# Lightning attention, a Fourier mix and an MLP on one core: the sign of the weights by a bit operation of VectorE, copies of the first batch in another order, and another figure behind the second batch's folds

## The chip, the core and the metric

The kernel runs on one core of a Trainium2 chip. The core has a matrix engine (TensorE, PE in the profile), an elementwise engine (VectorE, DVE), an engine for functions and copies (ScalarE, ACT), a general engine (GpSimd, POOL), and a queue engine that issues DMA transfers (SyncE, SP). Each engine takes its own instructions in a fixed order; semaphores hold an instruction back until what it needs is there. The metric is the time of one execution on the device, in microseconds (us); lower is better. The kernel before has a median of 832.36 us over 6 runs, from 827.09 to 833.14.

## The reference: what is computed

Four sequences (batches) of 768 positions pass through two blocks. The first is lightning attention with 8 heads of 64 elements: within a block of positions, scores with a decay by distance, and between blocks a state that is carried on.

```python
intra = np.einsum('bhic,bhjc->bhij', qb, kb) * Dmask[None]
intra = np.einsum('bhij,bhjd->bhid', intra, vb)
inter = np.einsum('bhid,bhde->bhie', qb * lam_pow[None], kv_state)
out[:, :, sl] = intra + inter
```

Its result, 768 rows of 512 elements for each batch, goes through a Fourier transform along both axes, of which the real part is added. Then come a normalisation of each row, an MLP from 512 to 2048 and back to 512, and a sum:

```python
mixed = np.real(np.fft.fft(np.fft.fft(x, axis=1), axis=2)).astype(np.float32)
u = x + mixed
un = (u - mu) / np.sqrt(var + 1e-06)
ch = np.maximum(un @ w_ch1, 0.0) @ w_ch2
return (u + ch).astype(np.float32)
```

The two weights arrive as float64 numbers (they are scaled by a float64 number when they are made), all else as float32. All matrix products here are in float32.

## The kernel before

**Attention.** For each batch `b` there are six chunks of 128 positions. `attn_in` loads k, q and v of a chunk, turns k and q with TensorE (L274, L279), and ScalarE copies them out of PSUM as kT and qT (L276, L281). `attn_out` makes the scores (L298), multiplies them by the decay on VectorE (`sc`, L302), and adds the state's part (L328) and the scores' part (L332) into one PSUM tile `po`. ScalarE copies it to `oT` (L335), and the function `back` turns it once more (L348) into rows, which ScalarE copies to `x` in two halves (L350, L351, the second half of the columns in reversed order).

The Fourier mix needs each row together with the row that mirrors it. For batches 1 to 3 the rows are written to memory (`xa`, `xb`) and gathered back in mirrored order by GpSimd (`mirror_a`, `mirror_b`). For batch 0 (`TURNED`) the mirrored rows are made on the chip: ScalarE copies `po` reversed along the positions into `oTs` (a tile named `ds`, L386, and one column at L392), and `mirrored` sends that through `back` too. `LEADS = (0,)` names the batch whose mix runs beside the next batch's attention.

**The Fourier mix.** `fold_a` and `fold_b` (L418 to L476) use the symmetries: sums and differences of mirrored rows and columns on VectorE, in place, in tiles `fe` and `fo`. The products with the tables of cosines and sines are L508 (along the positions) and L521 to L526 (along the columns). VectorE adds them to x (L588 to L592); then the norm (L538 to L556) gives `un`, which is turned by TensorE (L561) for the first four groups of rows or by VectorE for the others.

**The MLP.** A group is 256 rows. The first four groups (`PLAIN`) use `mlp`: the first product is L625 (four matmuls for each of 16 column blocks `fc`), a relu alternates between VectorE (L631, odd `fc`) and ScalarE (L633, even `fc`), and the second product is L639, one matmul for each `fc` and each 128 rows. Both products write to PSUM tiles of a pool `pm` with three buffers. The first three groups are done in two halves of `fc`, the second after the second half of the weights has come. The other eight groups are done in pairs from about 440 us on (`late`, L712 and L759).

**The weights.** `load_weights` takes one of 32 tiles of 128 × 512. It loads the 64-bit numbers as pairs of 32-bit words (`raw`) and makes float32 of them: the power of two out of the top 16 bits, `top`, which lie 8 bytes apart (L217 on VectorE, L218 on ScalarE), the sign (L216 on ScalarE, and a product L220 on VectorE), and the fraction (L222, L224). L225 multiplies the two. The order is: first half of w1 (tiles 0 to 7), first half of w2 (8 to 15), then the second halves.

**The order of the work.** Every part is a generator that yields an estimated time. `weave` and `beside` interleave two of them in proportion to these times: attention of batch 0 beside the first weights; the mix of batch 0 beside the attention of batch 1 and more weights; then the first MLP halves beside the weights and `fr`, the rest of the front end (attention and mix of batches 1 to 3). A larger yield in `fr` means that more MLP work is put in at that place. A scheduler then orders each engine's instructions, except those marked with `tc.keep_in_program_order`. TensorE takes its matmuls in the order so fixed: one that waits holds up all behind it.

```python
half = [[mlp(b, g, h * FO // 2, (h + 1) * FO // 2) for b, g in PLAIN[:3]] for h in range(2)]
fr = chain([att1, fft_ln(1)] + [front(b) for b in range(2, B)])
...
run(beside(beside(chain(half[0]), t_half, w, 0.5 * NW), t_half + 0.5 * NW, fr, t_rest * t_half / t_back))
run(w)
back = chain(half[1] + [mlp(*PLAIN[3])])
run(weave(fr, back, (t_back - t_half) / (t_rest - t_rest * t_half / t_back)))
```

Of the kernel before, what the change touches and what calls it, by code (L numbers as in the profile page):

```python
# [76 lines left out]
def kernel(  # L77
# [24 lines left out]
    BLK = [128, S // 4 + 1 - 128]  # L102
# [12 lines left out]
    def front_pool(name, bufs):  # L115
        return front_end.enter_context(tc.tile_pool(name=name, bufs=bufs, side="left"))
# [8 lines left out]
    fp = front_pool("fp", 1)  # L125
    np_ = front_pool("np", 2)
    ep = front_pool("ep", 2)
# [63 lines left out]
    WP = 512  # L191
# [8 lines left out]
    def load_weights(dst, src):  # L200

        if src.dtype == F32:
            nc.sync.dma_start(dst, src)
            return
        raw = hp_.tile([128, 2 * WP], U32, tag="hr", name=f"raw{cnt[0]}")
        e = ep.tile([128, 2 * WP], U16, tag="e", name=f"e{cnt[0]}")
        pw, sg = e[:, 0:WP], e[:, WP:2 * WP].bitcast(BF16)
        cnt[0] += 1
        nc.sync.dma_start(raw, src.bitcast(U32))
        lo, hi = raw[:, 0:2 * WP:2], raw[:, 1:2 * WP:2]  # L210
        top = raw.bitcast(U16)[:, 3:4 * WP:4]
        d = dst.bitcast(U32)


        pin = tc.keep_in_program_order if late_words else lambda i: i
        pin(nc.scalar.activation(sg, top.bitcast(I16), AF.Sign))  # L216
        pin(nc.vector.tensor_scalar(pw, top, 0x7FF0, None, op0=ALU.bitwise_and))  # L217
        nc.scalar.activation(pw, pw, AF.Relu, bias=cvt[:, 0:1], scale=8.0)  # L218
        p = pw.bitcast(BF16)
        nc.vector.tensor_tensor(p, p, sg, op=ALU.mult)  # L220

        pin(nc.vector.tensor_scalar(d, hi, 0x000FFFFF, 0x00100000, op0=ALU.bitwise_and, op1=ALU.bitwise_or))  # L222
        del late_words[0:1]
        nc.vector.scalar_tensor_tensor(dst, lo, 2.0 ** -32, d, op0=ALU.mult, op1=ALU.add)  # L224
        nc.vector.scalar_tensor_tensor(dst, dst, 2.0 ** -20, p, op0=ALU.mult, op1=ALU.mult)  # L225
# [28 lines left out]
    ins, oTs, eo = {}, {}, {}  # L254
    LEADS = (0,)
    TURNED = (0,)
    first = const.tile([128, HP, 1], F32, name="first")
# [31 lines left out]
    def attn_out(b, c, head):  # L289
        kT, qT, qs, kd, vt = ins.pop((b, c))  # L290
        last = c == NC - 1


        mm = nc.tensor.matmul
        pss = [psum_a([C, HP, C]) for _ in range(2)]
        for hp in range(HP):
            for hi in range(2):
                mm(pss[hi][:, hp, :], lhsT=kT[HD[hi], hp, :], rhs=qT[HD[hi], hp, :], start=True, stop=True)  # L298
        sc = []
        for hi in range(2):  # L300
            t = new(at, [C, HP, C], "sc", bufs=3)
            nc.vector.tensor_tensor(t, pss[hi], decay[:, hi::2, :], op=ALU.mult)  # L302
            sc.append(t)
        if last and b - 1 in LEADS:
            mirror_a(b, pin=True)
        yield 1.5


        s_old, s_new = st[(c + 1) % 2], st[c % 2]
        if not last:  # L310
            pu = psum_a([128, HP, D])
            for hp in range(HP):
                for hi in range(2):
                    h = 2 * hp + hi
                    mm(pu[HD[hi], hp, :], lhsT=kd[:, h, :], rhs=vt[:, h, :], start=True, stop=True)  # L315
            if c == 0:
                nc.vector.tensor_copy(s_new, pu)
            else:
                nc.gpsimd.tensor_tensor(s_new, s_old, spow.broadcast_to([128, HP, D]), op=ALU.mult)
                nc.vector.tensor_tensor(s_new, s_new, pu, op=ALU.add)  # L320
            yield 0.9


        po = psum_a([128, HP, C])
        if c > 0:
            for hp in range(HP):
                for hi in range(2):
                    mm(po[HD[hi], hp, :], lhsT=s_old[HD[hi], hp, :], rhs=qs[HD[hi], hp, :],  # L328
                       start=(hp == 0), stop=False, skip_group_check=True)
        for hp in range(HP):  # L330
            for hi in range(2):
                mm(po[HD[hi], hp, :], lhsT=vt[:, 2 * hp + hi, :], rhs=sc[hi][:, hp, :],  # L332
                   start=(c == 0 and hp == 0), stop=(hp == HP - 1), skip_group_check=True)
        oT = new(at, [128, HP, C], "oT")
        nc.scalar.copy(oT, po)  # L335
        if b in TURNED:

            if c == 0:
                nc.scalar.copy(first, po[:, :, 0:1])
            elif c > 1:  # L340
                nc.scalar.copy(oTs[b][:, :, 0:1], po[:, :, 0:1])
        yield 2.0
        yield from head

        def back(oT, x, n=128):
            px = psum_a([C, HP, 128])
            for hp in range(HP):
                nc.tensor.transpose(px[:, hp, :], oT[:, hp, :], ident)  # L348
            px = px.rearrange("p h e -> p (h e)")
            nc.scalar.copy(x[0:n, 0:HM], px[0:n, 0:HM])  # L350
            nc.scalar.copy(x[0:n, HM:DM], px[0:n, DM - 1:HM - 1:-1])  # L351

        if b not in TURNED:
            x = xn_[b, c] = new(xp, [C, DM], "x") if c < HC else new(xn, [C, DM], "xn")
            back(oT, x)
            if c == 0:
                xd[b] = (dram.tile([S - 256, DM], F32, name=f"xa{b}"), dram.tile([257, DM], F32, name=f"xb{b}"))
                nc.scalar.dma_start(xd[b][1][256:257], x[0:1])
            elif not last:
                nc.scalar.dma_start(xd[b][0][(c - 1) * C:c * C], x)  # L360
            if c >= NC - 2:
                nc.scalar.dma_start(xd[b][1][(c - NC + 2) * C:(c - NC + 3) * C], x)
            if c == NC - 2 and b - 1 not in LEADS:
                mirror_a(b)
            elif last:
                mirror_b(b)
            yield 1.7
            return


        if c == 2:
            eo[b] = new_eo()

        def mirrored(m):
            if m < HC:
                back(oTs[b], eo[b][HC - 1 - m][1][:, 1, 0:DM], BLK[HC - 1 - m])
            else:
                u = xs[b, HC + NC - 1 - m] = new(xp, [128, DM], "x")
                back(oTs[b], u)

        if c > 1:
            mirrored(c - 1)
            yield 1.4
        if c > 0:
            oTs[b] = new(fp, [128, DM + 4], "ds")[:, 0:DM].rearrange("p (h c) -> p h c", h=HP)
            nc.scalar.copy(oTs[b][:, :, C - 1:0:-1], po[:, :, 1:C])  # L386
        if not last:
            x = xn_[b, c] = new(xp, [C, DM], "x") if c < HC else new(xn, [C, DM], "xn")
            back(oT, x)
            yield 1.7  # L390
        else:
            nc.scalar.copy(oTs[b][:, :, 0:1], first)  # L392
            mirrored(c)
            for t in range(HC):
                xs[b, t] = xn_.pop((b, t))
            yield 1.4
# [28 lines left out]
    def mirror_a(b, pin=False):  # L425

        xa = xd[b][0]

        eo[b] = new_eo()
        for a, n in enumerate(BLK):  # L430
            i = gather(out=eo[b][a][1][0:n, 1, 0:DM], out_offset=None, in_=xa[:, :], in_offset=row_of(a, n))
            if pin:

                tc.keep_in_program_order(i)
        for t in range(2, HC):
            u = xs[b, HC + t] = new(xp, [128, DM], "x")
# [46 lines left out]
    def fft_ln(b):  # L483
# [7 lines left out]
        if b in LEADS:  # L491
            yield from fold_a(b)
            yield from fold_b(b, sets)
            yield 2.0
        else:
            yield 1.0
            run(fold_a(b))
            yield 3.0
            run(fold_b(b, sets))
            yield 9.0  # L500


        for i in range(5):
            ps = psum_a([128, 2, NK])
            m = 128 if i < 4 else 1
# [72 lines left out]
        for t in (1, 2, 0):  # L578
# [7 lines left out]
            ds = new(fp, [128, 2 * (HM + 2)], "ds")  # L586
# [3 lines left out]
            u, v_ = xs[b, t], xs[b, HC + t]  # L590
# [219 lines left out]
    def run(gen):  # L810
        return sum(gen)
# [35 lines left out]
    back = chain(half[1] + [mlp(*PLAIN[3])])  # L847
# [47 lines left out]
```

## Time and profile before

| what | value |
|---|---|
| time, median of 6 runs | 832.36 us (827.09 to 833.14) |
| the profiled execution: its own time | 833.46 us |
| its span in the profile | 831.3 us |
| TensorE busy | 799.9 us, 96% |
| VectorE busy | 443.2 us, 53% |
| ScalarE busy | 182.7 us, 22% |
| GpSimd busy | 77.9 us, 9% |
| L216, the sign on ScalarE | 32 of 683 ns: 21.8 us |
| L220, the product on VectorE | 32 of 440 ns: 14.1 us |

The profile is of one execution. Its span is the time from the first to the last instruction; the execution's own time has 2.2 us more around it. A share is the busy time of an engine over the whole span; the slices of the span show where that time lies. A row of a group gives the source line, the engine, the operation, what it writes and reads, the shapes, how many there are, their busy time and the mean of one, and then how long the engine stood still just before them and what ended that. A float32 matmul leaves two records in the trace. The mean of one instruction holds its latency; where instructions follow one another, the distance from one start to the next is shorter, and it is that which fills an engine.

### The profile page before, as it was taken

The numbers are of one execution on the slowest core, as the hardware profiler recorded it, in microseconds if no ns is written. First come the engines' busy times: TensorE is split into PE (matmuls) and PEld (weight loads), VectorE is DVE, ScalarE is ACT, GpSimd is POOL, SyncE is SP. The second block draws the span as 40 slices with busy tenths as digits, with TensorE's granted clock in tenths as the row PEclk, the third lists the DMA queues.
The fourth block names the chain that finished last, engine by engine and source line by source line (L and its number), as shares of the span: only waits on it lengthen the run. The fifth ranks groups of instructions, "written<-read, shape, count | busy, mean of one in ns | idle before, by whom it ended". The sixth has DMA issues, their size and how long they took to land.

```text
span 831.3 us, 11682 instructions
## 1 busy us (share of the span) xinstructions
PE 799.9 (96%) x4608; PEld 636.4 (77%) x4608; DVE 443.2 (53%) x1030; ACT 182.7 (22%) x436; POOL 77.9 (9%) x102
## 2 busy tenths in 40 slices
PE   6889889999999999999999999999999999999998
PEld 5767765757675866767748888888888888888886
DVE  6889779856843582245895551156312561145411
ACT  3655443125530210222101210022001220012100
POOL 3112140012010110220100000000000000000000
PEclk9999999999999999999999999999999999999999
DMA  9966542247861128440442011100111001110010
GB/s 235 252 149 194 142 132 76 84 113 186 229 168 41 51 55 161 104 123 22 114 105 98 1 51 51 51 1 0 52 51 51 0 1 35 36 32 1 1 39 25
DMA packets 126684, 68.87 MB, mean 83 GB/s; under 512 B 111151, under 2 KB 112175, under 8 KB 126631
## 3 DMA queue, kind: packets, MB, share of 16 engines
q1 hardware_dynamic: 121488, 55.67, 26.5%
q0 software_dynamic: 2112, 6.69, 2.5%
q10 hardware_dynamic: 3030, 5.78, 2.0%
q8 instruction: 36, 0.59, 0.3%
q14 instruction: 18, 0.14, 0.1%
HBM read 48.72 MB, written 19.40 MB: 82 GB/s over the span
## 4 chain that ended last, share of the span: by engine, by line
PE 80%; DVE 10%; DMA 4%; issue 4%; ACT 1%; POOL 1%; SPq 0%; POOLq 0%; DVEq 0%; ACTq 0%
PE p L759 23%; PE p L712 23%; PE pm L639 10%; PE pm L625 7%; PE pa L508 3%; PE pa L332 3%; PE pa L298 3%; PE pa L328 2%; DMA x<-xb,ix 1%; PE pa L274 1%; PE pa L315 1%; PE pa L348 1%; DMA xb<-xn 1%; DVE stt L538 1%; PE pa L279 1%
## 5 line engine op out<-in xcount | busy, mean ns | idle before, releaser
L625 PE MATMUL pm<-ut,w 128*128 128x256 f32 x512 | 119.1, 382 | 0.2 <-DVE hr L631 0.2
L639 PE MATMUL pm<-w,hr 128*128 128x512 f32 x256 | 118.0, 605 | 1.3 <-DVE hr L631 1.3
L625 PEld LDWEIGHTS pm<-ut,w 128*128 128x128 f32 x512 | 94.4, 190 | 15.4 <-issue 3.1
L712 PE MATMUL p<-ur,w 128*128 128x256 f32 x384 | 93.8, 379 | 0.0
L639 PEld LDWEIGHTS pm<-w,hr 128*128 128x128 f32 x256 | 46.9, 191 | 51.0 <-issue 47.6
L712 PEld LDWEIGHTS p<-ur,w 128*128 128x128 f32 x384 | 73.0, 190 | 10.3 <-issue 0.5
L712 PE MATMUL p<-us,w1s 128*128 128x256 f32 x256 | 65.7, 379 | 0.0
L759 PE MATMUL p<-w,hs 128*128 128x256 f32 x256 | 58.0, 379 | 0.5 <-DVE y L780 0.5
L759 PE MATMUL p<-w,ha 128*128 128x256 f32 x256 | 57.9, 379 | 0.0
L759 PE MATMUL p<-w2s,hs 128*128 128x256 f32 x256 | 57.9, 379 | 0.0
L759 PEld LDWEIGHTS p<-w,hs 128*128 128x128 f32 x256 | 48.5, 190 | 7.5 <-DVE y L780 0.9
L759 PEld LDWEIGHTS p<-w,ha 128*128 128x128 f32 x256 | 48.6, 190 | 6.6
L759 PEld LDWEIGHTS p<-w2s,hs 128*128 128x128 f32 x256 | 48.6, 190 | 6.6
L712 PEld LDWEIGHTS p<-us,w1s 128*128 128x128 f32 x256 | 48.6, 190 | 6.6
L614 POOL DMA_INDIRECT out_dram<-y,ix x12 | 11.8, 987 | 408.5 <-DVE y L785 341.8
L739 ACT COPY ha<-p 128x256 f32<-128x256 f32 x32 | 11.9, 372 | 169.1 <-PE p L712 139.4
L332 PE MATMUL pa<-sc,v 128*64 128x128 f32 x384 | 31.6, 282 | 6.6 <-DVE sc L302 6.6
L302 DVE TENSOR_TENSOR sc<-pa,decay 128x512 f32<-128x512 f32 x48 | 31.3, 681 | 12.4 <-PE pa L298 12.3
L750 DVE TENSOR_TENSOR ha<-p,ha 128x256 f32<-128x256 f32 x32 | 13.6, 424 | 44.9 <-ACT ha L749 44.9
L298 PEld LDWEIGHTS pa<-qT,kT 64*128 64x128 f32 x384 | 26.5, 195 | 12.1 <-ACT qT L281 5.4
L332 PEld LDWEIGHTS pa<-sc,v 128*64 128x64 f32 x384 | 22.9, 137 | 15.4 <-DVE sc L302 10.4
L298 PE MATMUL pa<-qT,kT 64*128 64x128 f32 x384 | 31.3, 296 | 2.5 <-ACT qT L281 2.2
(144 smaller groups left out, 1133.5 us busy)
## 6 DMA issues: line engine op xcount, KB each, us to landing
raw<-in_moe_w_ch_dram SPq DMA_DIRECT2D x32, 512.0 KB, 5.2
k<-in_k_dram SPq DMA_DIRECT2D x24, 256.0 KB, 4.8
q<-in_q_dram SPq DMA_DIRECT2D x24, 256.0 KB, 4.8
v<-in_v_dram SPq DMA_DIRECT2D x24, 256.0 KB, 4.2
ud<-x SPq DMA_DIRECT2D x16, 256.0 KB, 2.3
utd<-e SPq DMA_DIRECT2D x64, 64.0 KB, 2.2
u<-ud SPq DMA_DIRECT2D x16, 256.0 KB, 2.7
ur<-utd SPq DMA_DIRECT2D x6, 512.0 KB, 4.8
```

The costliest lines, as they stand in the source:

```text
L298: mm(pss[hi][:, hp, :], lhsT=kT[HD[hi], hp, :], rhs=qT[HD[hi], hp, :], start=True, stop=True)
L302: nc.vector.tensor_tensor(t, pss[hi], decay[:, hi::2, :], op=ALU.mult)
L328: mm(po[HD[hi], hp, :], lhsT=s_old[HD[hi], hp, :], rhs=qs[HD[hi], hp, :], start=(hp == 0), stop=False, skip_group_check=True)
L332: mm(po[HD[hi], hp, :], lhsT=vt[:, 2 * hp + hi, :], rhs=sc[hi][:, hp, :], start=(c == 0 and hp == 0), stop=(hp == HP - 1), skip_group_chec ...
L508: mm = nc.tensor.matmul(ps[0:m, n, :], lhsT=piece(a, i, n), rhs=cs[0:rows, a, i in (2, 3), n, :], start=(a == 0), stop=(a == 1))
L614: nc.gpsimd.indirect_dma_start(out=out.rearrange("b s d -> (b s) d"), out_offset=row_of(2 + HC * (b + 1) + T - HC), in_=y[:, :], in_offset ...
L625: nc.tensor.matmul(ps, lhsT=w1[:, c, 128 * fc:128 * fc + 128], rhs=ut[:, c, :], start=(c == 0), stop=(c == KO - 1))
L639: nc.tensor.matmul(ps, lhsT=hr[(fc - f0) // 4][:, fc % 4, 128 * i:128 * i + 128], rhs=w2[:, fc, :], start=(fc == f0), stop=(fc == f1 - 1))
L712: nc.tensor.matmul(ps, lhsT=s2.A[a][:, kt, 128 * i:128 * i + 128], rhs=U[b][:, kt, :], start=(first and kt == 0), stop=(kt == 1), skip_gro ...
L739: nc.scalar.copy(a11, two(X))
L750: V.tensor_tensor(a22, two(Z), a22, op=ADD)
L759: nc.tensor.matmul(ps, lhsT=h[a][:, s, i, :], rhs=s2.B[b][:, i, :], start=(first and i == 0), stop=(i == HF - 1), skip_group_check=True)
```

## The change

There are three parts. The sign: ScalarE's Sign and VectorE's bf16 product are taken out, and one operation of VectorE takes the top bit of the 16-bit words (`top & 0x8000`) and sets it in the power of two (`| pw`). It comes after ScalarE's Relu. The first batch's copies: `back` is split into the turning (`turn`) and the copying (`put`); in `attn_out` of batch 0 the earlier chunk's mirrored rows are turned first, then the reversed copy of `po` is made, in program order, and only then are the mirrored rows copied out. The folds: the figure that `fft_ln` yields after the folds of batch 1 is 12.0 where it was 9.0; for batches 2 and 3 it stays 9.0.

```diff
--- before.py
+++ after.py
@@ -203,8 +203,7 @@
             nc.sync.dma_start(dst, src)
             return
         raw = hp_.tile([128, 2 * WP], U32, tag="hr", name=f"raw{cnt[0]}")
-        e = ep.tile([128, 2 * WP], U16, tag="e", name=f"e{cnt[0]}")
-        pw, sg = e[:, 0:WP], e[:, WP:2 * WP].bitcast(BF16)
+        pw = ep.tile([128, 2 * WP], U16, tag="e", name=f"e{cnt[0]}")[:, 0:WP]
         cnt[0] += 1
         nc.sync.dma_start(raw, src.bitcast(U32))
         lo, hi = raw[:, 0:2 * WP:2], raw[:, 1:2 * WP:2]
@@ -213,11 +212,10 @@
 
 
         pin = tc.keep_in_program_order if late_words else lambda i: i
-        pin(nc.scalar.activation(sg, top.bitcast(I16), AF.Sign))
         pin(nc.vector.tensor_scalar(pw, top, 0x7FF0, None, op0=ALU.bitwise_and))
         nc.scalar.activation(pw, pw, AF.Relu, bias=cvt[:, 0:1], scale=8.0)
+        nc.vector.scalar_tensor_tensor(pw, top, 0x8000, pw, op0=ALU.bitwise_and, op1=ALU.bitwise_or)
         p = pw.bitcast(BF16)
-        nc.vector.tensor_tensor(p, p, sg, op=ALU.mult)
 
         pin(nc.vector.tensor_scalar(d, hi, 0x000FFFFF, 0x00100000, op0=ALU.bitwise_and, op1=ALU.bitwise_or))
         del late_words[0:1]
@@ -342,13 +340,18 @@
         yield 2.0
         yield from head
 
-        def back(oT, x, n=128):
+        def turn(oT):
             px = psum_a([C, HP, 128])
             for hp in range(HP):
                 nc.tensor.transpose(px[:, hp, :], oT[:, hp, :], ident)
-            px = px.rearrange("p h e -> p (h e)")
+            return px.rearrange("p h e -> p (h e)")
+
+        def put(px, x, n=128):
             nc.scalar.copy(x[0:n, 0:HM], px[0:n, 0:HM])
             nc.scalar.copy(x[0:n, HM:DM], px[0:n, DM - 1:HM - 1:-1])
+
+        def back(oT, x):
+            put(turn(oT), x)
 
         if b not in TURNED:
             x = xn_[b, c] = new(xp, [C, DM], "x") if c < HC else new(xn, [C, DM], "xn")
@@ -371,26 +374,29 @@
         if c == 2:
             eo[b] = new_eo()
 
-        def mirrored(m):
+        def mirrored(m, px):
             if m < HC:
-                back(oTs[b], eo[b][HC - 1 - m][1][:, 1, 0:DM], BLK[HC - 1 - m])
+                put(px, eo[b][HC - 1 - m][1][:, 1, 0:DM][0:BLK[HC - 1 - m]], BLK[HC - 1 - m])
             else:
                 u = xs[b, HC + NC - 1 - m] = new(xp, [128, DM], "x")
-                back(oTs[b], u)
-
+                put(px, u)
+
+        px = turn(oTs[b]) if c > 1 else None
+        if c > 0:
+
+            oTs[b] = new(fp, [128, DM + 4], "ds")[:, 0:DM].rearrange("p (h c) -> p h c", h=HP)
+            tc.keep_in_program_order(nc.scalar.copy(oTs[b][:, :, C - 1:0:-1], po[:, :, 1:C]))
+        if last:
+            tc.keep_in_program_order(nc.scalar.copy(oTs[b][:, :, 0:1], first))
         if c > 1:
-            mirrored(c - 1)
+            mirrored(c - 1, px)
             yield 1.4
-        if c > 0:
-            oTs[b] = new(fp, [128, DM + 4], "ds")[:, 0:DM].rearrange("p (h c) -> p h c", h=HP)
-            nc.scalar.copy(oTs[b][:, :, C - 1:0:-1], po[:, :, 1:C])
         if not last:
             x = xn_[b, c] = new(xp, [C, DM], "x") if c < HC else new(xn, [C, DM], "xn")
             back(oT, x)
             yield 1.7
         else:
-            nc.scalar.copy(oTs[b][:, :, 0:1], first)
-            mirrored(c)
+            mirrored(c, turn(oTs[b]))
             for t in range(HC):
                 xs[b, t] = xn_.pop((b, t))
             yield 1.4
@@ -497,7 +503,7 @@
             run(fold_a(b))
             yield 3.0
             run(fold_b(b, sets))
-            yield 9.0
+            yield 12.0 if b - 1 in LEADS else 9.0
 
 
         for i in range(5):
```

More of the change, by code (lines that the diff above doesn't have):

```diff
@@ L372, in attn_out @@
             eo[b] = new_eo()
-        def mirrored(m):
+        def mirrored(m, px):
             if m < HC:
-                back(oTs[b], eo[b][HC - 1 - m][1][:, 1, 0:DM], BLK[HC - 1 - m])
+                put(px, eo[b][HC - 1 - m][1][:, 1, 0:DM][0:BLK[HC - 1 - m]], BLK[HC - 1 - m])
             else:
                 u = xs[b, HC + NC - 1 - m] = new(xp, [128, DM], "x")
-                back(oTs[b], u)
-        if c > 1:
-            mirrored(c - 1)
-            yield 1.4
+                put(px, u)
+        px = turn(oTs[b]) if c > 1 else None
         if c > 0:
             oTs[b] = new(fp, [128, DM + 4], "ds")[:, 0:DM].rearrange("p (h c) -> p h c", h=HP)
-            nc.scalar.copy(oTs[b][:, :, C - 1:0:-1], po[:, :, 1:C])
+            tc.keep_in_program_order(nc.scalar.copy(oTs[b][:, :, C - 1:0:-1], po[:, :, 1:C]))
+        if last:
+            tc.keep_in_program_order(nc.scalar.copy(oTs[b][:, :, 0:1], first))
+        if c > 1:
+            mirrored(c - 1, px)
+            yield 1.4
         if not last:
```

## The prediction

> **What bounds the kernel now.** I read the page first, for the share of each engine, then the busy times by stretch, then the waits of TensorE (PE), and last the order in time around the largest wait. From the page:
>
> ```profile
> PE 799.9 (96%) x4608; PEld 636.4 (77%) x4608; DVE 443.2 (53%) x1030; ACT 182.7 (22%) x436; POOL 77.9 (9%) x102
> PE   6889889999999999999999999999999999999998
> DVE  6889779856843582245895551156312561145411
> PE 80%; DVE 10%; DMA 4%; issue 4%; ACT 1%; POOL 1%; SPq 0%; POOLq 0%; DVEq 0%; ACTq 0%
> ```
>
> TensorE works 799.9 of 831.3 us. A change can only win from the 31 us in which it stands still, nearly all of them in the first seven slices of 20.8 us, where VectorE (DVE) is nearly full; or it can add to them. The busy times by stretch (from:to, length, then PE, PEld, DVE, ACT, POOL, granted TensorE clock, DMA share, GB/s):
>
> ```profile
> 21.00:42.00 21.00, 18.05 (x229) 15.07 (x229) 17.60 (x34) 13.79 (x32) 4.03 (x4) 1.00 1.00 251
> 42.00:63.00 21.00, 17.57 (x191) 13.58 (x189) 16.84 (x33) 11.00 (x28) 4.00 (x4) 0.92 0.69 153
> 63.00:84.00 21.00, 19.19 (x204) 15.46 (x203) 20.90 (x44) 11.25 (x23) 4.57 (x5) 1.00 0.66 181
> 122.00:126.00 4.00, 1.13 (x4) 0.28 (x2) 3.27 (x9) 0.20 (x1) 0.00 (x0) 1.00 0.22 74
> 126.00:131.00 5.00, 4.80 (x9) 2.29 (x10) 5.00 (x15) 0.20 (x1) 0.00 (x0) 0.66 0.00 0
> ```
>
> From 63 to 84 us VectorE has 0.1 us to spare, so there each microsecond added to it is late work. After the hole at 122 us the clock is only 0.66: a hole costs TensorE its own length and then a spell at half speed. The waits of TensorE, first from 21 to 63 us, then from 105 to 168 us (total, times, longest):
>
> ```profile
> PE pa L332 <- DVE sc L302: 3.4, 3, 1.3
> PE pa L348 <- ACT ds L392: 1.3, 1, 1.3
> ```
>
> ```profile
> PE pa L508 <- DVE fe L467: 3.1, 1, 3.1
> PE pa L561 <- DVE un L556: 1.7, 2, 1.0
> ```
>
> Around the third, the order in time of both engines (start, length; a matmul has two records, so x2 is one matmul):
>
> ```profile
> 122.11 1.02 PE L639 MATMUL pm<-w,hr 128*128 128x512 f32 x2
> 126.20 0.56 PE L508 MATMUL pa<-cs,fe 128*128 128x193 f32 x2 [3.07 <-DVE fe L467]
> 126.61 4.35 PE L639 MATMUL pm<-w,hr 128*128 128x512 f32 x6
> ```
>
> ```profile
> 122.73 0.69 DVE L418 TENSOR_TENSOR fe<-x,x 128x512 f32<-128x512 f32 x1 [2.97 <-DMA x<-xb,ix]
> 132.22 0.42 DVE L476 TENSOR_TENSOR fo<-fo 65x256 f32<-65x256 f32 x1
> 132.56 0.68 DVE L224 SCALAR_TENSOR_TENSOR w<-raw,w 128x512 f32<-128x512 uint32 x1
> 133.16 0.42 DVE L631 TENSOR_SCALAR hr<-pm 128x256 f32<-128x256 f32 x1
> ```
>
> The second batch's gather lands at 122.73, the folds hold VectorE until 132.5, and TensorE fills that time by taking Fourier products (L508) and second MLP products (L639) in turn. By 149.1 us it has done 16 L639, 20 L508 and one group of L521 to L526. From there on it hardly stops, so lateness here is carried to the end.
>
> [...] the two-source bf16 product L220, contiguous, takes 440 ns, the two-source float32 L225 726 ns, and the single-source L217 with a strided input 460 ns. The new operation has two sources, one with a step of four. [...] The trace shows three such spells at 0.50 (52.4, 93.5 and 127.5 us, 3.4 us each), but already after windows that were 57%, 51% and 38% busy; a window 58% busy, from 69.5 us, brought none. [...] in the trace, too, the relu L631 runs only after the folds ahead of it.
>
> **The change part by part.** *The sign.* The rows concerned (busy, mean ns, idle before):
>
> ```profile
> L225 DVE SCALAR_TENSOR_TENSOR w<-w,e 128x512 f32<-128x512 f32 x32 | 23.2, 726 | 0.4
> L217 DVE TENSOR_SCALAR e<-raw 128x512 uint16<-128x512 uint16 x32 | 14.7, 460 | 4.5 <-DMA raw<-in_moe_w_ch_dram 4.5
> L220 DVE TENSOR_TENSOR e<-e 128x512 bf16<-128x512 bf16 x32 | 14.1, 440 | 7.8 <-ACT e L218 5.8 <-ACT e L216 2.0
> ```
>
> ```profile
> L216 ACT ACTIVATE e<-raw 128x512 bf16<-128x512 int16 x32 | 21.8, 683 | 16.1 <-DMA raw<-in_moe_w_ch_dram 14.0 <-ACT x L351 0.8 <-DVE w L225 0.7
> ```
>
> ScalarE loses 32 × 0.683 = 21.8 us. VectorE swaps a 440 ns product for a bit operation that no row shows. Below it is bounded by L220's price (no change), above by L225's; I take the upper[...]. Counted from one start to the next this is 0.60 (L224, 132.56 to 133.16) for 0.34, so +0.26 us a tile and 8.4 us on VectorE. Nearly half the tiles convert after 150 us, where VectorE has slack (10.3 busy of 21 from 168 to 189 us): cost nothing, and up to 0.26 × 14 = 3.6 if that cover were gone.
>
> In the first chunks the absent Sign lets ScalarE copy qT sooner, and in the built program's order one L302 no longer stands behind an L217 that waits until 23.7 for its tile. That L302 starts about 24.4 instead of 26.1; limited by ScalarE's next copies, I take 1.3 us of the 3.4. DMA is full until 42 us, so the gain can be as low as 0.
>
> Four tiles convert from 75 to 87 us, where VectorE is full (11.86 busy of 12): 4 × 0.26 = 1.0 us later for L588 and the scores behind it. One more tile lies on the chain near 106 us: 0.3. Loss 1.3 (0 at L220's price).
>
> *The reversed copy.* L386 and L392 are pinned ahead of L350 and L351, so the transposes L348 that waited 1.3 us for L392 get their input two half-copies sooner, about 0.65 us. The copies L350 and L351 move behind it; what reads them (eo, from 60 us) has time. Then the window from 49.0 us is busier than 57%, and the half-speed spell at 52.4 (3.4 us, up to 1.7 lost) may not come; [...] I count half, 0.8. Sum of the early stage: 1.3 + 0.65 + 0.8 = 2.7 (0 to 3.7).
>
> *The 12.0.* More of the MLP is given out between the folds and the first L508. In the built program TensorE then has five L639 in a row (0.86 each, from 122.1 to 126.4), and next the first L639 of the other row tile. It reuses the PSUM tile that the relu L631 reads, and that relu stands on VectorE behind all folds. By the rows above: the folds lose one product and one L222 and gain one bit operation (−0.34 − 0.34 + 0.60), so the last starts at 132.14; L222 0.34, then the relu, done at 133.25. TensorE stands from 126.4 to 133.25, 6.9 us in place of 3.1. The next L639 need w2 tiles 13, 14 and 15: tile 13 is ready at about 134.75. Tile 14 has L217, ScalarE's 0.72, the bit operation, L224, a relu and L225 in a row: 137.5. Tile 15: 140.0. All L508 come after these, so no longer fill the gaps. At full clock the five are done at 140.9. After two windows nearly empty the clock is at half until about 141, which adds up to 1.7: 142.6. Left are 20 L508 at 0.33 (6.6), five L639 (4.3) and an L521 group (1.1): 154.6, against 149.1. Loss 5.5; 3.8 without the cold spell, 2.5 if the gather lands 1.3 us sooner against TensorE, 6.5 with a longer spell.
>
> *Later.* The same interleaving shifts what follows. In the third batch one L639 waits 1.3 us for a relu that now stands earlier: +0.5 (−1 to 1.3). In the fourth, five groups of L625 instead of three stand ahead of the first L508, which waited 1.6 us in two waits with 0.3 around them: +1.8 (0 to 1.9). From 440 us on nothing is changed.
>
> Sum: 2.7 − 1.3 − 5.5 + 0.5 + 1.8 = 1.8 us slower. The profiled execution took 833.46 us (span 831.3); it becomes 835.3. It stood 1.1 above the median of the runs, 832.36, so the forecast for the median is **834.2**, main case 831 to 837.
>
> **The rivals.** *Slower.* The early and late gains do not reach the end: DMA is at 1.00 to 42 us, so chunk 3 may wait for its k instead, and the fourth batch's folds may wait for their gather. Left are 1.3 + 5.5 = 6.8: 839.2; with a second cold spell 841. For it speaks that the empty stretch at 126 us follows from a fixed order on two engines. It decides where the early and late gains together stay under 2.6 us. *Faster.* The five products fill the old hole: this is so if the gather lands about 6 us sooner against TensorE, because a freed ScalarE writes the second batch's rows earlier, and then the relu is past when TensorE needs it. The loss is then 0, and 2.7 − 1.3 + 2.3 = 3.7 remains, with the other half of the cold spell 4.5: 827.8. It counts as faster once the loss is below about 0.3. Against it: ScalarE works only 8.2 of 21 us from 105 to 126, so Sign hardly delays those rows. *Nothing.* The bit operation costs no more than the product, and TensorE's other work covers the rest: 832.4; against it stands the order.
>
> **How the numbers follow.** Main case 0.47, slower 0.33, faster 0.12, nothing 0.08. About 0.5% (4.2 us) is what a measurement can tell from no change: 828.2 to 836.5. Faster is the third case with an edge of the first: 0.14. Slower is the second with the main case's upper edge: 0.39. The rest, 0.47, is the same. The range leaves out the lower part of the faster case and the double cold spell's end: 828.5 to 841.5.
>
> **What would show it.** The row of the bit operation near 720 ns (at 440 the early losses go). In the third slice, L332's wait for L302 down from 3.4 to about 2, and none of L348 on L392. A clock of 1.00 from 52 to 56 us. At the second batch's folds one wait of L639 for the relu near 7 us, two for L225 of about 0.7 and 1.9, and none of L508 for L467; a clock of 0.5 after it. In the fourth batch no wait for L467. I am wrong if that large wait is under 3 us, if the chunks before 50 us do not end sooner, or if a stage past 160 us stands still where it did not.

## The result: 0.7% slower

The changed kernel has a median of 837.93 us over 17 runs (835.02 to 842.61), the kernel before beside it 832.26 us over 38 runs (826.53 to 837.75). The ratio is 1.0071, with a 95% interval from 1.0054 to 1.0087. The difference, 5.7 us, is beyond the 4.2 us that the prediction named as the limit of what can be told from no change. It went the way of the forecast, slower, but lies above the main case (831 to 837) and close to the case called *slower* (839.2).

The profiled execution of the changed kernel took 836.33 us, with a span of 834.6 us. It is 2.9 us above the profiled execution of before, not 5.7: that one was 1.1 us above its median, and this one is 1.6 below its own. The two profiles therefore show only about half of the difference; the rest has to be looked for in further profiles below.

The busy times of the changed kernel, first line of the page:

```profile
PE 799.7 (96%) x4608; PEld 636.1 (76%) x4608; DVE 451.5 (54%) x1030; ACT 164.6 (20%) x404; POOL 79.8 (10%) x102
```

TensorE has the same work. VectorE has 8.3 us more (foretold: 8.4), ScalarE 18.1 less. The row of the bit operation:

```profile
L217 DVE SCALAR_TENSOR_TENSOR e<-raw,e 128x512 uint16<-128x512 uint16 x32 | 23.2, 725 | 3.4 <-ACT e L216 3.4
```

725 ns is the price of the float32 operation with two sources (L225 before: 726 ns), not that of the 16-bit product (L220 before: 440 ns). Now TensorE's waits in the changed kernel, from 21 to 63 us, from 63 to 105 us (with the line of the kernel before below it), and from 105 to 168 us (total, times, longest):

```profile
PE pa L330 <- DVE sc L300: 1.9, 3, 1.3
PE pa L296 <- ACT qT L279: 1.6, 2, 1.3
PE pa L346 <- ACT ds L390: 1.1, 1, 1.1
```

```profile
PE pa L330 <- DVE sc L300: 3.7, 3, 2.9
```

```profile
PE pa L332 <- DVE sc L302: 2.3, 3, 1.5
```

```profile
PE pm L645 <- DVE hr L637: 6.8, 1, 6.8
PE pa L567 <- DVE un L562: 1.7, 2, 0.9
PE pm L645 <- DVE w L223: 0.7, 2, 0.5
```

In the first stretch the wait for the scores fell from 3.4 to 1.9 us, but a wait of 1.3 us for qT is new, and the wait for the reversed copy fell only from 1.3 to 1.1. In the second, the longest wait for the scores is 2.9 us; before it was 1.5 there. In the third, the wait of L508 for the fold is gone and one of 6.8 us for a relu stands in its place. In order of time, first TensorE and then VectorE at the second batch's folds:

```profile
121.57 4.46 PE L645 MATMUL pm<-w,hr 128*128 128x512 f32 x10
132.85 3.49 PE L645 MATMUL pm<-w,hr 128*128 128x512 f32 x4 [6.82 <-DVE hr L637]
136.86 2.84 PE L645 MATMUL pm<-w,hr 128*128 128x512 f32 x6 [0.52 <-DVE w L223]
139.91 1.12 PE L645 MATMUL pm<-w,hr 128*128 128x512 f32 x2 [0.21 <-DVE w L223]
140.87 2.79 PE L514 MATMUL pa<-cs,fe 128*128 128x193 f32 x16
```

```profile
121.95 0.69 DVE L424 TENSOR_TENSOR fe<-x,x 128x512 f32<-128x512 f32 x1 [2.90 <-DMA x<-xb,ix]
131.70 0.42 DVE L482 TENSOR_TENSOR fo<-fo 65x256 f32<-65x256 f32 x1
132.04 0.42 DVE L220 TENSOR_SCALAR w<-raw 128x512 uint32<-128x512 uint32 x1
132.37 0.42 DVE L637 TENSOR_SCALAR hr<-pm 128x256 f32<-128x256 f32 x1
```

Five second products end at 126.0; the folds end at 132.1, the relu behind them at 132.8, and TensorE goes on at 132.85. The Fourier products L514 are in TensorE's order behind all of this. In the kernel before the first of them ran 3.5 us after the first fold began (126.20 and 122.73), so here it could have run from about 125.5 us on (my estimate from these two numbers). The busy times by stretch (PE is the second number after the stretch; the granted clock stands before the last two):

```profile
63.00:84.00 21.00, 19.19 (x198) 15.42 (x197) 20.96 (x43) 9.85 (x22) 3.93 (x4) 1.00 0.78 214
126.00:131.00 5.00, 0.03 (x1) 0.00 (x0) 5.00 (x14) 0.92 (x2) 0.00 (x0) 0.81 0.00 0
131.00:137.00 6.00, 3.63 (x5) 1.27 (x6) 5.80 (x13) 0.72 (x1) 0.00 (x0) 0.59 0.38 96
```

The empty stretch is followed by two windows of the clock at half speed, 0.50 from 129.1 to 135.9 us; before there was one there (0.50 from 127.6 to 130.8). At 52 us, where the kernel before had one (0.51 from 52.4 to 55.8), there is none (1.00).

### The profile page after: what moved, and what is told of

It is laid out like the page before. It is cut to its first block, busy times and chain, and to the rows that moved or that the text cites. A ratio compares the mean times of both kernels' runs of the same rounds, so it can differ in the third digit from the quotient of the medians.

```text
span 834.6 us, 11642 instructions
## 1 busy us (share of the span) xinstructions
PE 799.7 (96%) x4608; PEld 636.1 (76%) x4608; DVE 451.5 (54%) x1030; ACT 164.6 (20%) x404; POOL 79.8 (10%) x102
## 4 chain that ended last, share of the span: by engine, by line
PE 78%; DVE 13%; issue 4%; DMA 3%; ACT 1%; POOL 1%; SPq 0%; POOLq 0%; DVEq 0%; ACTq 0%
PE p L765 23%; PE p L718 23%; PE pm L645 10%; PE pm L631 7%; PE pa L330 3%; PE pa L296 2%; PE pa L514 2%; PE pa L326 1%; DMA raw<-in_moe_w_ch_dram 1%; PE pa L272 1%; DMA x<-xb,ix 1%; PE pa L346 1%; DVE sc L300 1%; PE pa L313 1%; PE pa L277 1%
## 5 line engine op out<-in xcount | busy, mean ns | idle before, releaser
L631 PE MATMUL pm<-ut,w 128*128 128x256 f32 x512 | 118.6, 382 | 0.1
L631 PEld LDWEIGHTS pm<-ut,w 128*128 128x128 f32 x512 | 94.4, 190 | 15.2 <-issue 3.5
L330 PE MATMUL pa<-sc,v 128*64 128x128 f32 x384 | 33.5, 289 | 7.3 <-DVE sc L300 7.2
L216 ACT ACTIVATE e<-e,cvt 128x512 uint16<-128x512 uint16 x32 | 23.1, 723 | 54.7 <-DVE e L215 54.7
```

The lines of the kernel that those rows point to most:

```text
L631: nc.tensor.matmul(ps, lhsT=w1[:, c, 128 * fc:128 * fc + 128], rhs=ut[:, c, :], start=(c == 0), stop=(c == KO - 1))
```

## The experiments

Two theories. *Order*: the loss is where the relu stands on VectorE, and that nothing TensorE could do stands ahead of what waits for it. *Load*: the loss is the 8.3 us that VectorE works more. All figures are medians; the kernel before measured 832.45, 832.33 and 832.85 us beside the three groups of runs. The ratio is worked out from the runs and is not the quotient of the two medians, so the two can differ by 0.1%. Each edit also lets the scheduler put other instructions in another order, so a run can change more than the line that it names.

| what | median us | ratio to before (95%) |
|---|---|---|
| the bit operation alone | 833.78 | 1.0015 (1.0001 to 1.0029) |
| 12.0 alone | 834.39 | 1.0020 (1.0008 to 1.0032) |
| the change with 9.0 | 833.49 | 1.0001 (0.9988 to 1.0014) |
| the change, relus on ScalarE | 832.57 | 1.0002 (0.9980 to 1.0023) |
| bit operation and 12.0 | 839.71 | 1.0086 (1.0061 to 1.0110) |
| copies and 12.0 | 834.11 | 1.0023 (1.0008 to 1.0039) |
| the change with 10.5 | 833.24 | 1.0013 (0.9992 to 1.0033) |
| the change, relus on ScalarE, 15.0 | 831.35 | 0.9989 (0.9973 to 1.0005) |
| the change, gathers issued twice | 834.07 | 1.0027 (1.0009 to 1.0045) |
| copies, relus on ScalarE, 15.0, old sign | 828.85 | 0.9957 (0.9940 to 0.9973) |
| copies, relus on ScalarE, 12.0, old sign | 829.47 | 0.9966 (0.9949 to 0.9982) |

### One part at a time

The bit operation alone: the kernel before with

```diff
-        pin(nc.scalar.activation(sg, top.bitcast(I16), AF.Sign))
...
+        nc.vector.scalar_tensor_tensor(pw, top, 0x8000, pw, op0=ALU.bitwise_and, op1=ALU.bitwise_or)
...
-        nc.vector.tensor_tensor(p, p, sg, op=ALU.mult)
```

> The kernel before with the bit operation alone. Theory (the loss is the order of TensorE at the second batch's folds): that order keeps L508 between the second products, so its wait there stays near 3 us; about 1 us is won in the chunks and 1.3 lost near 90 us: 831 to 833.5. Rival (the extra 8.4 us of VectorE are the loss): 836 to 838, nearly the whole difference.

12.0 alone: the kernel before with

```diff
-            yield 9.0
+            yield 12.0 if b - 1 in LEADS else 9.0
```

> The kernel before with 12.0 in place of 9.0 alone. Theory: one wait of the second product for the relu of 6.5 to 7.5 us at the folds in place of the 3.1 us wait of L508, 5 us lost there, 2 won in the fourth batch: 835 to 838. Rival (VectorE's load): 831 to 833, as the bit operation is absent.

The changed kernel with 9.0 put back:

```diff
-            yield 12.0 if b - 1 in LEADS else 9.0
+            yield 9.0
```

> The changed kernel with 9.0 put back. Theory: no wait for the relu at the folds, one of about 3 us for the fold; 830.5 to 833, the copies adding some 0.5 us of gain to the bit operation alone. Rival (VectorE's load): 836 to 838.

Load as the whole cause is out: with the bit operation and all of VectorE's additional work, but 9.0, the kernel is within 0.15% of before. Both kernels with the bit operation and 9.0 came out a little above the ranges expected (833.78 for 833.5, 833.49 for 833). But neither does 12.0 alone make the difference: 834.39, a little under the range that theory *order* gave. Its profile has the wait for the relu, but shorter (TensorE's waits from 105 to 168 us):

```profile
PE pm L639 <- DVE hr L631: 4.0, 1, 4.0
```

### The relu's place

The relus of the first half group (`PLAIN[0]`) all go to ScalarE, the rest is the changed kernel:

```diff
-            if fc % 2:
+            if fc % 2 and not ((b, g) == PLAIN[0] and f0 == 0):
```

> The changed kernel, 12.0 kept, with the relus of the first half group all on ScalarE, so that none of them stands behind the folds on VectorE. Theory: the 6.8 us wait for the relu goes, ten second products run in a row, and a wait for the weights of tile 13 of about 3.8 us takes its place: 3 us less than the changed kernel, 834 to 836. If instead it stays at 838, the wait for the relu was not what set the time.

832.57 us, 5.4 less than the changed kernel and under the range expected. The waits of this kernel from 105 to 168 us:

```profile
PE pa L567 <- DVE un L562: 1.7, 2, 0.9
PE pm L645 <- DVE w L223: 0.3, 1, 0.3
```

TensorE runs twelve second products in a row instead of five (24 records, two for each):

```profile
120.94 10.73 PE L645 MATMUL pm<-w,hr 128*128 128x512 f32 x24
```

When the tenth of them ends, at about 129.6 us, tile 13 is just ready (its L223 ends at 129.64); the expected wait of 3.8 us for it is not in this profile. (In this execution, 825.65 us, the clock was not lowered within the span, 1.000; its other runs go from 826.5 to 837.0.)

The next kernel leaves the relu on VectorE and makes the rows land *later*: the two gathers are issued twice.

```diff
-            gather(out=u[:, :], out_offset=None, in_=xd[b][1][:, :], in_offset=row_of(2 + t))
+            for _ in range(2 if b == 1 else 1):
+                gather(out=u[:, :], out_offset=None, in_=xd[b][1][:, :], in_offset=row_of(2 + t))
```

> The changed kernel with the two gathers of the second batch's rows issued twice. The folds then start later, and in the built order the relu of the fifth column block and the weights of tile 13 stand ahead of the folds on VectorE, still on VectorE. Theory (the place of the relu decides): no wait for the relu, ten second products in a row through the folds, 831 to 835 although the rows land later. Rival (the landing of the rows decides, the relu's place does not): later by the extra gathers, 839 to 842.

In the built order the scheduler, with more time to fill, put the relu ahead of the folds. Tile 13 is not complete before the folds, as I had expected: its last step, L223, stands among them, and only parts of the conversions (L222, L217) went ahead. VectorE, then TensorE, in order of time:

```profile
121.54 0.42 DVE L638 TENSOR_SCALAR hr<-pm 128x256 f32<-128x256 f32 x1
128.42 0.69 DVE L424 TENSOR_TENSOR fe<-x,x 128x512 f32<-128x512 f32 x1 [4.93 <-DMA x<-xb,ix]
132.33 0.69 DVE L223 SCALAR_TENSOR_TENSOR w<-w,e 128x512 f32<-128x512 f32 x1
```

```profile
133.08 7.10 PE L646 MATMUL pm<-w,hr 128*128 128x512 f32 x12 [4.30 <-DVE w L223]
```

The rows land at 128.4 instead of 121.95, 6.5 us later, and the kernel is faster than the changed one: 834.07 against 837.93. The wait for the relu is gone. Six second products run in a row and not the ten expected, and then a wait of 4.3 us for the weights of tile 13 is left. The late rows alone, then, do not make the kernel slow, and the number of the rival (839 to 842) is out. As other instructions moved with the relu, it is this run together with the one before that speaks for the relu's place.

With 10.5 instead of 12.0 (the same line of the code) most L514 stand ahead of the product that waits for the relu:

> The changed kernel with 10.5: four second products run before the first L514, and most L514 stand ahead of the product that waits for the relu. Theory (the relu's wait costs because nothing that is ready stands before it): the wait for the relu is gone or under 1 us, the waits are for the folds again, 831 to 834. If any extra second product ahead of L514 costs: 835 to 837.

833.24 us, as expected in size. The folds' wait is back, in two pieces of 2.7 us in all, and no wait for the relu appears in that stretch:

```profile
PE pa L514 <- DVE fe L473: 2.7, 2, 2.4
```

### Which two parts go together badly

The single parts add up to 2 or 3 us and not to 5.7. The pairs (their edits are those above and the copies of the change):

> Bit operation and 12.0, the copies as before. The parts do not add up so far: the sign alone gave +1.3 us, 12.0 alone +1.9, both with the copies +5.7. Theory (with the bit operation behind ScalarE's Relu the weights of tiles 13 and 14 come later after the folds, so the wait for the relu is followed by waits for weights): 836 to 838.5, with one wait for the relu and one or two for L223. Rival (the copies do it, by shifting the second batch's gather): 833 to 835.

> Copies and 12.0, the sign as before. Theory: as 12.0 alone, 833 to 835, no wait for weights at the folds. Rival (the copies): 836 to 838.5.

The bit operation is the partner: 839.71 with it, 834.11 with the old sign. The copies do nothing that can be measured: 834.11 against 834.39 without them, and with the bit operation 837.93 against 839.71, where the two intervals overlap and the second kernel has only six runs. But the mechanism that I expected is not the one: the wait for weights after the relu was 0.2 us with the bit operation. The waits of *copies and 12.0*, then of *bit operation and 12.0*, from 105 to 168 us:

```profile
PE pm L647 <- DVE hr L639: 7.1, 1, 7.1
```

```profile
PE pm L637 <- DVE hr L629: 3.9, 1, 3.9
PE pa L559 <- DVE un L554: 2.1, 3, 0.9
PE pm L637 <- DVE w L223: 0.2, 1, 0.2
```

The slower kernel has the shorter wait. In these two profiles its loss lies earlier: it reaches the folds' first second product at 128.46, *copies and 12.0* at 119.77. I therefore compared this moment in all profiles. With the bit operation (nine profiles) it is 121.6, 124.1, 124.8, 122.7, 120.9, 128.5, 124.8, 123.4 and 123.5, mean 123.8. With the old sign (five, that of before first) it is 122.1, 122.6, 119.8, 123.1 and 119.1, mean 121.3. The difference of 2.5 us is only about twice its standard error (1.1 us), since each group is spread widely. Most of the spread is the clock: up to this moment it was at half speed for 3.4, 10.2, 10.2, 6.8, 0, 17.1, 10.2, 6.8 and 3.4 us in the nine, and for 6.8, 6.8, 3.4, 6.8 and 0 us in the five. A straight line through all 14 gives 0.43 us for each us at half speed, and 1.2 us (standard error 0.4) for the bit operation at equal clock. The other half of the 2.5 us is that the nine were at half speed for longer, 7.6 us on average against 4.8.

The 1.2 us can be seen directly. Between the second scores L302 at 71.1 us and those at 91.5 us (kernel before), an execution without a spell at half speed in this stretch takes 20.44 or 20.45 us with the old sign (three profiles) and 21.67 to 21.69 with the bit operation (five): 1.24 us more, each time. TensorE's wait for the scores near 91 us is 2.9 us in all nine and 1.5 in the five. VectorE in order of time, from 84.8 us in the changed kernel, then from 86.9 us in the kernel before:

```profile
84.89 0.69 DVE L283 TENSOR_TENSOR qs<-pa,qpow 128x512 f32<-128x512 f32 x1
85.50 0.68 DVE L223 SCALAR_TENSOR_TENSOR w<-w,e 128x512 f32<-128x512 f32 x1
...
87.49 1.55 DVE L598 TENSOR_TENSOR x<-x,ds 128x512 f32<-128x512 f32 x1
88.96 1.27 DVE L544 BATCH_NORM_STATS2 stt<-x 128x6 f32<-128x512 f32 x2
...
90.90 0.65 DVE L300 TENSOR_TENSOR sc<-pa,decay 128x512 f32<-128x512 f32 x1
```

```profile
86.94 0.69 DVE L285 TENSOR_TENSOR qs<-pa,qpow 128x512 f32<-128x512 f32 x1
87.58 0.43 DVE L588 TENSOR_TENSOR ds<-pa,bs 128x256 f32<-128x256 f32 x1
...
88.98 0.68 DVE L592 TENSOR_TENSOR x<-x,ds 128x512 f32<-128x512 f32 x1
...
91.53 0.66 DVE L302 TENSOR_TENSOR sc<-pa,decay 128x512 f32<-128x512 f32 x1
```

From qs to the second scores it is 6.0 us instead of 4.6, as one L223 more stands between them, 0.60 us, and one addition takes 1.55 instead of 0.68. The first of the two makes TensorE's wait longer without making the scores later, since that L223 stood ahead of qs before. The addition, 0.87 us, is most of the 1.24. GpSimd, changed kernel and kernel before:

```profile
87.19 1.29 POOL L268 TENSOR_TENSOR kd<-k,decay 128x512 f32<-128x512 f32 x1 [5.93 <-PE pa L313]
```

```profile
89.25 1.33 POOL L270 TENSOR_TENSOR kd<-k,decay 128x512 f32<-128x512 f32 x1 [6.38 <-PE pa L315]
```

In the changed kernel GpSimd's product starts 0.3 us ahead of the addition, which ends 0.55 after it; in the kernel before it starts 0.27 after the addition began, which is not held up. So it is in all nine profiles with the bit operation (the addition takes 1.54 or 1.55 us) and in none of the five (0.68 or 0.69). GpSimd's product, too, takes longer here than at the median of its 20: 1.29 us against 1.06 in the changed kernel, where it starts behind the addition L597, and 1.33 against 1.07 in the kernel before, where it starts behind L592. What holds the two engines up is not shown, and no run takes this alignment away by itself.

The rest differs from execution to execution and goes with the clock: in *bit operation and 12.0* it was at half speed from 29.7 to 36.6, 74.1 to 77.5 and 98.0 to 104.8 us, in *copies and 12.0* before the folds only from 68.8 to 72.2. That the bit operation brings these windows is not shown; it makes one wait of TensorE longer, and a spell at half speed began during that wait of 2.9 us or within 2 us after it in seven of the nine profiles (at 91.5 us in the changed kernel), after the wait of 1.5 us in two of the five (at 93.5 us in the kernel before).

This does not yet say why the bit operation and 12.0 cost more together than apart, for the 1.24 us are in the kernels with 9.0 too. The time from the first second product to the end of the span shows one more piece:

| profiles | us |
|---|---|
| 9.0: before; bit operation (two) | 709.2; 709.0, 709.1 |
| 12.0, old sign (two) | 708.9, 711.9 |
| 12.0, bit operation (three) | 710.5, 710.6, 713.0 |
| relus on ScalarE, 12.0: bit operation; old sign | 702.9; 706.8 |

The higher figure of the second and of the third row goes with a wait for the relu near 7 us, the others with one near 4. Like with like, the bit operation costs 1.1 to 1.7 us after this moment with 12.0, and nothing with 9.0. (In the last row the kernel with the bit operation is the shorter one: in its profile the rows came early, as the next profile below explains, and in the other there is a wait of 3.4 us for weights.) Where these are lost I have not followed further, and a part of the difference between 3.2 us (the parts added) and 5.7 stays open.

A second profile of the changed kernel:

> The changed kernel once more, for a second profile. If the wait for the relu is a matter of order, it is there again, at 4 us when GpSimd issues the first gather in about 1.1 us and at 7 when it takes over 3. The rest of the median's difference should show as one or two more windows of the clock at half speed before 122 us.

The wait came true, and so did two more windows at half speed; but at 836.42 us this execution, too, was under the median of 837.93. GpSimd's two issues of the gather, and TensorE's wait from 105 to 168 us:

```profile
117.82 1.22 POOL L450 DMA_INDIRECT x<-xb,ix  x1 [0.19 <-issue]
119.34 2.73 POOL L450 DMA_INDIRECT x<-xb,ix  x1 [0.30 <-issue]
```

```profile
PE pm L645 <- DVE hr L637: 3.8, 1, 3.8
```

In the first profile of the changed kernel they were:

```profile
116.00 3.69 POOL L450 DMA_INDIRECT x<-xb,ix  x1 [0.89 <-DMA xb<-xn]
119.99 0.95 POOL L450 DMA_INDIRECT x<-xb,ix  x1 [0.30 <-issue]
```

With the short first issue the rows are there sooner, and the wait is 3.8 and not 6.8 us. This execution had lost its time earlier: the clock was at half speed from 90.3 to 100.5 us (in the first profile from 91.5 to 95.0), and the folds' first second product came at 124.09. Both executions end up with the same span, 834.6.

### A version that beats both

First the relus on ScalarE with 15.0, so that L514 and products that wait for weights alternate:

> The relus of the first half group on ScalarE, and 15.0 in place of 12.0: nine second products, then L514 in turn with products that wait for the weights. Theory: TensorE has work through the folds, 829 to 832, less than both kernels. Rival (what is filled here is missing at the later batches): 832 to 835.

831.35, 6.6 below the changed kernel; against before the interval includes 1. Then with the old sign, at 15.0 and 12.0:

> Copies, relus of the first half group on ScalarE, 15.0, but the sign by ScalarE and the product as before. Theory (the bit operation loses about 1 us near 90 us and at the tiles after the folds, the filled folds gain): below the same with the bit operation (831.35), 828.5 to 831. If the bit operation's load were no loss: 831 to 833.

> As the last with 12.0. Theory: 829 to 832, below the same with the bit operation (832.57).

828.85 and 829.47: below both kernels, by 0.43% (0.27 to 0.60) and 0.34% (0.18 to 0.51) against before. The old sign is worth 2.5 us in one pair and 3.1 in the other (2.7 and 3.0 by the ratios, as these runs belong to different groups). TensorE's wait at the folds in the 12.0 version shows what is still to be had there:

```profile
PE pm L647 <- DVE w L225: 3.4, 1, 3.4
```

## Why the prediction was right, and where it was not

**Right.** The bit operation's price (the upper bound, taken as an estimate: 0.60 us from start to start, and 725 ns by the row; 8.3 us more on VectorE, where 32 × 0.26 is 8.3 and not the 8.4 written). The stall at the folds: 6.9 us foretold, 6.82 found in the first profile, by the relu, with no wait of L508 for L467. It depends on the gather's issue, which the prediction did not see: in the second profile it is 3.8. The half-speed spell after the folds (0.50 from 129.1 to 135.9 us); that every hole brings one is not shown, as the wait near 91 us brought one in seven of nine profiles. The direction, and the range; by the bound of 0.5% the result is slower, to which 0.39 was given, against 0.47 for the same.

**Mis-sized at the folds.** The step put the loss at 5.5. In the profile the same 16 second products, 20 Fourier products and one group of L527 to L532 are done at 154.86 with four matmuls of L631 (1.84 us) among them that did not count: 153.0 against 149.1, from a start 0.5 us sooner, so 4.4. The term was the half-speed spell: the sum has the second products ahead of L508 done at 140.9, and at 142.6 with 1.7 us for the half-speed clock on top; in the profile L514 starts at 140.87. While the clock was at half speed, to 135.9, VectorE made the tiles. Tile 13, for which 0.65 us was foretold, cost no wait; tile 14 cost 0.52 and not 1.9, and tile 15 cost 0.21:

```profile
133.64 0.69 DVE L223 SCALAR_TENSOR_TENSOR w<-w,e 128x512 f32<-128x512 f32 x1
136.12 0.68 DVE L223 SCALAR_TENSOR_TENSOR w<-w,e 128x512 f32<-128x512 f32 x1
139.16 0.69 DVE L223 SCALAR_TENSOR_TENSOR w<-w,e 128x512 f32<-128x512 f32 x1
```

The wait for weights and the slow clock overlap. (The sum also names five second products three times, one short of its own 16; six ran between the relu and L514.)

**Wrong in the early stage: the gain of 2.7.** It was to give the folds a start 1.4 us sooner, after a loss of 1.3. In the first profile of the changed kernel they start 0.5 us sooner, in the second 2.0 later, and in all nine profiles with the bit operation 1.7 later than in the profile of before on average. Term by term, by how much sooner the second scores of a chunk start in the first profile than in the kernel before: 0.9 us at 33 us and 0.6 at 47, where 1.3 and then 1.95 were foretold. The chunk at 30 us gained less because qT now waits for ScalarE's L216, which waits for VectorE, and the wait for the reversed copy fell by 0.2 and not 0.65. At 62 us it is 1.9, since the kernel before has its half-speed spell at 52 us and this one has none. Its absence was counted as a gain of 0.8 and came, but by luck and not by the change: the spell is missing in the profile of 12.0 alone as well, where the code up to the folds is that of before. By 91 us it is 0.6. So the loss near 90 us, 1.2 us for the 1.0 foretold, had the right size but another make: not 4 × 0.26, but mostly an addition that now meets GpSimd's product (0.87). And while I credited the clock with half a spell, an estimate, I did not charge the other side: the second profile has three windows at half speed from 90 us on.

**Too large later.** The sum gave 2.3 us back in the third and fourth batches. In the profile the lead of 0.54 us at the folds, less 4.4, would be 3.9 behind; it ends 3.2 behind, so 0.6 came back (2.8 behind at 440 us, and another 0.4 lost after it, where I had counted nothing). In this profile that is the largest miss: 1.7 us, against 0.9 in the early stage and 1.1, the other way, at the folds. The waits for L467 in the fourth batch are gone as foretold, but the changed kernel has a longer one for scores there, 1.6 us where the kernel before waits 0.7 (TensorE from 310 to 400 us):

```profile
PE pa L330 <- DVE sc L300: 1.6, 1, 1.6
```

The profile of 12.0 alone has the same wait of 1.6 us, so it comes with the 12.0. A stage past 160 us that stands still where it did not was one of the three signs named for being wrong, and it came: besides this wait there is one of 0.5 us near 174 us.

**The median.** Against the profiled executions I was 1.1 us off (1.8 foretold, 2.9 found), against the medians 3.8. My sum was made for one execution and shifted by a constant. The runs differ in the clock: the median granted clock is 0.992 in the changed kernel's runs and 0.996 in those of before, and 0.002 less goes with about 1.2 us more within the changed kernel's runs, and with 1.2 to 1.6 us within those of before. The step of 0.004 would then be 2.3 us or more of the missing 2.8. It is a correlation and not an experiment.

**The rivals.** *Slower* came nearest in time, and half of it happened: the early gain did not reach the end and the later gain was mostly taken by other waits. Its reason, DMA being full, was not it; TensorE's only wait for a load from 21 to 63 us is 0.2 us. It was to decide where the early and late gains together stay under 2.6 us, and in the first profile they were 1.1. *Nothing* is out, as the bit operation did cost more than the product. *Faster* asked for rows landing 6 us sooner; what it took was not sooner rows but another place for a relu.

## What to carry to other kernels

Giving TensorE, which takes its matmuls in the built order, "more work behind" a stall helped only where what was placed there was ready: here one product waited 6.8 us for its relu, and L514 behind it began at 140.87 us. Look at which PSUM buffer its first instruction reuses, and where the instruction that frees that buffer stands on its own engine. A cheap operation behind a long block of another engine is as late as the block: the relu of 0.42 us stood behind the folds until 132.37 us, and with the relus moved to ScalarE, 20% busy, the kernel was 5.4 us faster. And the kernels with the bit operation, which stands on an engine with no slack in one stage (VectorE 20.96 of 21 us from 63 to 84), lost 1.24 us between 71 and 91 us, though that engine is only 54% busy over the whole span; 0.87 of it lies in an addition that met a product of GpSimd. Count by stage, and look at what GpSimd will then run beside it. Treat a hole in TensorE's work as possibly longer than it is, since a spell at half speed may follow, as after the 6.8 us at the folds (0.50 to 135.9 us): in the stretch from 71 to 91 us one of 3.4 us cost 1.5 or 1.6 us. The two profiles of the changed kernel were at half speed for 10.2 and 17.1 us, so a difference of a few us between two profiles says little before the clock of both is looked at.

## What was not expected of the hardware

- **The issue of a gather on GpSimd has two lengths.** With two gathers in a row the first took 3.3 to 4.0 us and the second 0.95, or the first 1.1 to 1.2 and the second 2.6 to 2.7. In the first case the rows landed 9.3 to 9.7 us after the issue of the write that they wait for (before: 113.38 to 122.73), in the second the folds found them in time 6.3 to 6.5 us after it (12.0 alone: 113.91, fold at 120.23). The stall for the relu followed: 6.8 and 7.1 us with the long first issue, 3.8 to 4.0 with the short one, in five profiles. The same kernel showed both. Whether the long issue waits for VectorE is not shown; the traces speak for it only in part. In the kernel before VectorE's row of operations ends at 119.77 and the first issue at 120.39, in the changed kernel at 119.06 and 119.69, 0.6 us later in both. But in the second profile of the changed kernel the long issue ends at 122.07, while VectorE works on without a pause, so the end of the row is not what it waits for there. A run in which VectorE stands still meanwhile was not made, and what sets the length is open.
- **GpSimd against VectorE.** The addition that took 1.55 us instead of 0.68, above: in the 14 profiles the order of the two engines, 0.3 us one way or the other, goes with 0.87 us.
- **The clock.** The windows at half speed were 3.4 us or multiples of it, and their number varied between executions of one kernel: from none within the span (relus on ScalarE, 825.65 us, clock 1.000) to clocks of 0.990 (836.97 us). Of that kernel's 14 runs the clock explains most of the spread, 1.9 us for each 0.002. From 71 to 91 us the kernels with the bit operation take 21.7 us without such a spell and 23.3 with one of 3.4 us, those with the old sign 20.4, and 21.9 or 22.0.
